# Two places of their own for the output tiles of the last stage, a four-place weight ring, and an earlier split of the last block's rows

## The chip, the cores and the metric

The kernel runs on one core of a Trainium2 chip. The metric is device time in microseconds (us). Before the change three timed runs gave 866.95, 863.05 and 864.15, median 864.15.

## The reference, cut to what matters

The program is one chain: attention (a coarse one and a local one, summed), a mixture of eight experts with one expert per token, and a two-layer feed-forward. Only the last link is touched:

```python
# x: 2304 tokens x 512; w_in: 512 x 2048; w_out: 2048 x 512
h = x @ w_in
g = np.maximum(h, 0.0) + alpha * np.minimum(h, 0.0)
out = g @ w_out                       # 2304 x 512, float32
```

## The kernel before, in words

**Precision.** Each float32 operand is split in a high and a low part (`split`: ScalarE casts the high part, VectorE or GpSimd subtracts it), and a product is three matmuls, high*high, high*low, low*high.

**Blocks.** The last stage (`moe2`) takes the tokens in blocks 0 to 3 of 512 and block 4 of 256. For each of 16 slices f of the hidden width it makes h (128 hidden columns x tokens) in a PSUM bank, applies the activation on VectorE (`act`: two instructions over the bank, into a tile m), splits the result into gh and gl, and later multiplies these by w_out into Y, four PSUM tiles of 128 tokens x 512 (`second`, 12 matmuls of 512 columns per slice, queued in `queue` and taken out by `run`). Blocks 0 and 1 are `plain`, block 4 is `end`.

**Blocks 2 and 3** (`sevens`) use seven half-size products instead of eight. Two slices make a pair; pairs q = 0 to 15 run through both blocks, p = q mod 8. A pair has seven products of six matmuls of 256 columns, into three banks: A ("11", then "S2", "S3", "22" added in turn, ScalarE copying the bank out after each), B ("12") and C ("S1", then "S4" added). Their parts meet in two tiles h0 and h1, which are activated and split like the others; q5 holds a copy of C.

**The weight ring.** S1 to S4 are sums of parts of w_in. During block 1, `Split7.make` computes them for p = 0 to 7 (tiles S1m and so on) and writes them to DRAM (`sd`); `Split7.fetch` loads them for each pair (S1r and so on, 256 KB each). Both draw their tiles from one ring of five places (`ring`): place i mod 5, in the order S1, S2, S4, S3. So a tile takes the place of the tile five before it: S2r of pair 0 that of S1m of p = 7. SyncE issues stores and fetches in one queue, in order, and a fetch waits there until its place is free.

**The output.** When the last slice of a token tile is added, `leave` copies Y from PSUM to a tile o (even tiles ScalarE, odd ones VectorE), and GpSimd issues an indirect DMA that writes the 128 rows to their tokens. The four DMAs of a block run one after the other, each issued when the one before has landed. The o tiles come from `mt`, the ring "m" with four places, which also holds every m, h0, h1, ma and mb: after a block's end these find their places taken by o tiles until the DMAs land.

**Other tiles.** `c64` gives a staging tile of 128 x 256 in turn from pool `ep`, tag "L", and pool `wst`; q5 comes from it. `plain_x` splits the token rows of block 4 into xf. In the source it stands after all pairs, ahead of the last pair's last product; its places in xf are free when the last pair has done "12".

**What sets the order.** The source is not the order of the instructions: a scheduler with its own forecast of times orders them per engine, and each engine then runs its list in order. Names with a number (h0, oy) lose it in the rows of the trace.

Of the kernel before, what the change touches and what calls it, by code (L numbers as in the profile page):

```python
# [5 lines left out]
F32=mybir.dt.float32; F32R=mybir.dt.float32r; BF16=mybir.dt.bfloat16; I32=mybir.dt.int32; U32=mybir.dt.uint32  # L6
# [538 lines left out]
def split(nc, hi, lo, x, lo_engine):  # L545

    nc.scalar.copy(hi,x)  # L547
    return lo_engine.tensor_tensor(out=lo,in0=x,in1=hi.bitcast(F32),op=ALU.subtract)  # L548
# [198 lines left out]
SKEW=48  # L747
BLOCKS=[(512*j,512) for j in range(4)]+[(2048,256)]
SEVEN=(2,3)
# [38 lines left out]
def moe2(tc, stack, wp, tp, xf, ep, win, wst, c64, W2out, W2in, al, ysT, ytok, sd, out, first):  # L788
    nc=tc.nc
    op=stack.enter_context(tc.tile_pool(name="o_const",bufs=1))  # L790
# [5 lines left out]
    wir,wil=win  # L796
    nring=itertools.count()
    def ring(name):
        i=next(nring)%5
        pool,tag,n=(wst,"raw64",3) if i<3 else (op,"s2",2)  # L800
        return pool.tile([128,2,2,128],F32R,tag=tag,name=name,bufs=n)
    seven=Split7(tc,ring,sd,win)
    def mt(name): return wk.tile([128,512],F32,tag="m",name=name,bufs=4)
    def bank(i,name): return hp.tile([128,512],F32,tag=f"h{i}",name=name)
    def gtiles(j,f):
        return wk.tile([128,512],F32R,tag="gh",name=f"gh{j}_{f}",bufs=LAG+1),wk.tile([128,512],F32R,tag="gl",name=f"gl{j}_{f}",bufs=LAG+1)
    G0=[gtiles(0,0)]; M0=[mt("m0_0")]
    xk=wk.tile([128,XW],F32R,name="xk",bufs=1)
    xin={}; Y={}; queue=[]; numbers={0:first[1]}
    def run(n):  # L810
        for _ in range(min(n,len(queue))): queue.pop(0)()
    def second(j,t,f,gh,gl,ts=None):
        ts=slice(128*t,128*t+128) if ts is None else ts
        for k,(a,b) in enumerate(((gh,woh),(gh,wol),(gl,woh))):
            nc.tensor.matmul(Y[j][t],lhsT=a[:,ts],rhs=b[:,f],start=f==0 and k==0,stop=f==15 and k==2)  # L815
        if f==15: leave(j,t)
    def leave(j,t):
        o=mt(f"o{j}{t}"); ti=numbers[j]
        if t%2: nc.vector.tensor_copy(o,Y[j][t])
        else: nc.scalar.copy(o,Y[j][t])  # L820
        nc.gpsimd.indirect_dma_start(out=out[:],out_offset=bass.IndirectOffsetOnAxis(ap=ti[:,t:t+1],axis=0),in_=o[:],in_offset=None,bounds_check=N-1,oob_is_err=False)  # L821
    def follow(j,f,gh,gl):
        for t in range(4): queue.append(lambda t=t: second(j,t,f,gh,gl))
    def accum(j): Y[j]=[yp.tile([128,DM],F32,tag="y",name=f"oy{j}{t}") for t in range(BLOCKS[j][1]//128)]
    def act(f,g,m,h,n=512):
        nc.vector.tensor_scalar(out=m[:,:n],in0=h[:,:n],scalar1=0.0,scalar2=al[:,f:f+1],op0=ALU.min,op1=ALU.mult)  # L826
        nc.vector.scalar_tensor_tensor(out=g[:,:n],in0=h[:,:n],scalar=0.0,in1=m[:,:n],op0=ALU.max,op1=ALU.add)  # L827

    raws={}
    def load_x(j):  # L830
        r0,n=BLOCKS[j]
        a=ep.tile([128,2,512],F32,tag="eh",name=f"oTa{j}",bufs=1); b=[ep.tile([128,512],F32,tag=t,name=f"oT{t}{j}",bufs=1) for t in ("T","eo")]
        raws[j]=[a[:,0],a[:,1],b[0],b[1]]
        for c in range(4): tc.keep_in_program_order(nc.sync.dma_start(raws[j][c][:,:n],ysT[128*c:128*c+128,r0:r0+n]))
        numbers[j]=ti=row_numbers(tc,tp,ytok,j)
        return a
    def plain_x(j,x,at):
        n=BLOCKS[j][1]
        hi=x[:,at:at+4*n].rearrange("p (c t) -> p c t",c=4); lo=x[:,at+4*n:at+8*n].rearrange("p (c t) -> p c t",c=4)
        for c in range(4): split(nc,hi[:,c],lo[:,c],raws[j][c][:,:n],nc.vector)  # L840
        xin[j]=(hi,lo)
    def place(x,i): return x[:,512*i+SKEW:512*i+SKEW+512].rearrange("p (c t) -> p c t",c=2)
    PLACES={"11":(0,0),"21":(0,2),"T1":(0,4),"T2":(0,6),"22":(1,0),"T3":(1,2),"T4":(1,4)}
    def seven_x(j,a,name):
        R=raws[j]; t1=slice(0,256); t2=slice(256,512); two=nc.gpsimd.tensor_tensor
        x,i=PLACES[name]
        if name=="11" and j>SEVEN[0]: x,i=1,6
        hi,lo=place((xf,xk)[x],i),place((xf,xk)[x],i+1)
        if name=="T1": two(out=a[:,:,t1],in0=a[:,:,t2],in1=a[:,:,t1],op=ALU.subtract)
        if name=="T3":  # L850
            for c in range(2): two(out=a[:,c,t2],in0=R[2+c][:,t2],in1=a[:,c,t2],op=ALU.subtract)
        if name=="T2":
            for c in range(2): two(out=a[:,c,t1],in0=R[2+c][:,t2],in1=a[:,c,t1],op=ALU.subtract)
        if name=="T4":
            for c in range(2): two(out=R[2+c][:,t1],in0=R[2+c][:,t1],in1=a[:,c,t1],op=ALU.subtract)
        if name in ("11","T1","T2"): split(nc,hi,lo,a[:,:,t1],nc.vector)
        elif name=="T3": split(nc,hi,lo,a[:,:,t2],nc.vector)
        else:
            for c in range(2): split(nc,hi[:,c],lo[:,c],R[2+c][:,t2 if name=="22" else t1],nc.vector)
        xin[j,name]=(hi,lo)  # L860
# [31 lines left out]
    def product(q,p,j,w,x,o,start,stop):  # L892
        W=seven.weight(q if w in seven.SUMS else p,w); xh,xl=xin[j,x]
        k=0
        for c in range(2):
            for a,b in ((0,xh),(0,xl),(1,xh)):
                nc.tensor.matmul(o[:,:256],lhsT=W(a,c),rhs=b[:,c],start=start and k==0,stop=stop and k==5,skip_group_check=True); k+=1  # L897
    def sevens():
        last=None
        for q in range(8*len(SEVEN)):  # L900
            j=SEVEN[0]+q//8; p=q%8; nxt=j+1 if p==7 else None
            if p==0: accum(j)
            if q+1<8*len(SEVEN): seven.fetch(q+1,(q+1)%8)
            if p==4: held.append(load_x(j+1))
            def x_for(name,nxt=nxt):
                if nxt in SEVEN: seven_x(nxt,held[-1],name)
            A=bank(q%2,f"pA{q}"); B=bank(2,f"pB{q}"); C=bank(3,f"pC{q}")
            if p==6 and j+1 in SEVEN: seven_x(j+1,held[-1],"11")
            product(q,p,j,"11","11",A,True,False)
            h0=mt(f"h0{q}"); h1=mt(f"h1{q}"); q5=c64(f"q5{q}",[128,256])  # L910
            nc.scalar.copy(h0[:,:256],A[:,:256])
            if last: last()
            run(4)
            product(q,p,j,"12","21",B,True,True)
            nc.vector.tensor_tensor(out=h0[:,:256],in0=B[:,:256],in1=h0[:,:256],op=ALU.add)
            x_for("21")
            product(q,p,j,"S1","T1",C,True,False)
            nc.scalar.copy(q5,C[:,:256])
            x_for("T1")
            product(q,p,j,"S2","T2",A,False,False)  # L920
            nc.scalar.copy(h0[:,256:],A[:,:256])
            x_for("T2")
            run(2)
            product(q,p,j,"S4","22",C,False,True)
            nc.vector.tensor_tensor(out=h0[:,256:],in0=C[:,:256],in1=h0[:,256:],op=ALU.add)
            gh,gl=gtiles(j,2*p)
            act(2*p,h0,mt(f"ma{q}"),h0); split(nc,gh,gl,h0,nc.vector); follow(j,2*p,gh,gl)
            x_for("22")
            product(q,p,j,"S3","T3",A,False,False)
            nc.scalar.copy(h1[:,256:],A[:,:256])  # L930
            nc.vector.tensor_tensor(out=h1[:,256:],in0=q5,in1=h1[:,256:],op=ALU.add)
            x_for("T3")
            run(2)
            def last(q=q,p=p,j=j,A=A,h1=h1,x_for=x_for):
                product(q,p,j,"22","T4",A,False,True)
                nc.scalar.copy(h1[:,:256],A[:,:256])
                gh,gl=gtiles(j,2*p+1)
                act(2*p+1,h1,mt(f"mb{q}"),h1); split(nc,gh,gl,h1,nc.vector); follow(j,2*p+1,gh,gl)
                x_for("T4")
        j=SEVEN[-1]+1  # L940
        plain_x(j,xf,SKEW)
        last(); run(4)
    def end(j):
        r0,n=BLOCKS[j]; xh,xl=xin.pop(j); accum(j); ts=slice(0,128); H=[]
# [14 lines left out]
        for f in range(16): second(j,1,f,zh[:,f],zl[:,f],ts)  # L959
    xin[0]=first[0]  # L960
    plain(0); plain(1); sevens(); end(4)

def row_numbers(tc, tp, ytok, j):
# [8 lines left out]
def body(tc,q,k,v,mod,wg,bias,w1,w2,w_in,w_out,alpha,out):  # L972
    nc=tc.nc
    with ExitStack() as ctx:
# [91 lines left out]
        with ExitStack() as s2:  # L1066
            moe2(tc,s2,wp,rp,xf,ep,(wir,wil),wst,c64,W2out,lambda f: W2in(24+f,1),al,ysT,ytok,sd,out,first)
# [26 lines left out]
```

## Time and profile before

| what | value |
|---|---|
| median of three runs | 864.15 us (863.05 to 866.95) |
| profiled execution | 859.76 us |
| its span, first to last instruction | 858.0 us |
| PE busy | 798.7 us (93%) |
| VectorE, ScalarE, GpSimd busy | 582.4, 402.7, 227.0 us (68%, 47%, 26%) |
| mean granted TensorE clock | 0.981 |

PE is TensorE's matmuls, DVE VectorE, ACT ScalarE, POOL GpSimd, SPq SyncE's queue of DMA issues. A busy PE is an engine that has a matmul in flight.

### The profile page before, as it was taken

What the parts mean: (1) busy time and instruction counts of PE and PEld (TensorE: products, weight loads), DVE (VectorE), ACT (ScalarE), POOL (GpSimd) and SP (SyncE); (2) the same over time, 40 slices, a digit from 0 to 9 for tenths busy, and PEclk for the clock granted to TensorE, in tenths of its full rate; (3) what the DMA queues carried; (4) which work ended last, traced back from release to release, by engine and by line L of the source; (5) the groups of instructions that cost most, each with busy time, mean ns of one, the idle gap of its engine ahead of it and who ended that gap; (6) DMA issues with size and microseconds to landing.
All of it is one profiled execution on the core that took longest, in us unless ns stands there. A gap on an engine that the chain in (4) does not pass through costs nothing.

```text
span 858.0 us, 18117 instructions
## 1 busy us (share of the span) xinstructions
PE 798.7 (93%) x6535; PEld 699.9 (82%) x6535; DVE 582.4 (68%) x1489; ACT 402.7 (47%) x987; POOL 227.0 (26%) x420
## 2 busy tenths in 40 slices
PE   4799899999998999989999999999999999899996
PEld 3477777778898999989998877788888988799895
DVE  6866856547525789988849999598845565445472
ACT  7697786885422665665532232233323233233220
POOL 9425556347431001101002224433410110100010
PEclk9989999989999999999999999999999999999999
DMA  7645675322313533469203343133262533342000
GB/s 193 170 109 159 190 217 148 90 53 56 80 52 87 88 100 84 94 124 285 83 26 118 116 159 112 74 144 126 99 228 92 160 109 113 103 119 87 13 38 25
DMA packets 110439, 96.99 MB, mean 113 GB/s; under 512 B 41992, under 2 KB 85512, under 8 KB 110344
## 3 DMA queue, kind: packets, MB, share of 16 engines
q1 hardware_dynamic: 107368, 86.19, 36.2%
q0 software_dynamic: 2976, 9.59, 3.2%
q8 instruction: 53, 0.87, 0.5%
q14 instruction: 42, 0.34, 0.2%
HBM read 93.21 MB, written 27.29 MB: 140 GB/s over the span
## 4 chain that ended last, share of the span: by engine, by line
PE 24%; DVE 14%; issue 14%; DMA 10%; ACT 2%; POOL 1%; SPq 1%; POOLq 0%; DVEq 0%; ACTq 0%
PE oy L815 7%; PE h L719 5%; PE y L739 5%; DMA out<-o,tt 5%; PE pA L897 3%; DMA wo<-in_moe_w_out 2%; PE oh L951 2%; DVE m L826 2%; DMA L<-xs 1%; DVE gl L548 1%; DVE m L827 1%; PE pC L897 1%; DVE sa L778 1%; DMA oTa<-ysT 1%; DVE w1l L548 1%
## 5 line engine op out<-in xcount | busy, mean ns | idle before, releaser
L815 PE MATMUL oy<-woh,gh 128*128 128x512 f32 x272 | 104.9, 394 | 6.5 <-ACT gh L547 3.3
L815 PE MATMUL oy<-wol,gh 128*128 128x512 f32 x272 | 106.4, 391 | 0.8 <-POOL wol L548 0.8
L815 PE MATMUL oy<-woh,gl 128*128 128x512 f32 x272 | 96.6, 390 | 0.0
L719 PE MATMUL h<-xh,w1h 128*128 128x256 f32 x224 | 63.5, 284 | 6.8 <-DVE hl L722 6.8
L815 PEld LDWEIGHTS oy<-woh,gh 128*128 128x128 f32 x272 | 50.9, 188 | 18.0 <-ACT woh L547 4.9
L719 PE MATMUL h<-xh,w1l 128*128 128x256 f32 x224 | 63.1, 282 | 0.0
L719 PE MATMUL h<-xl,w1h 128*128 128x256 f32 x224 | 63.1, 282 | 0.0
L547 ACT CAST gh<-m 128x512 fp32r<-128x512 f32 (+1 forms) x48 | 24.7, 514 | 80.3 <-DVE m L827 78.1
L739 PE MATMUL y<-hh,w2h 128*128 128x256 f32 x224 | 61.0, 280 | 0.0
L739 PE MATMUL y<-hh,w2l 128*128 128x256 f32 x224 | 60.5, 280 | 0.0
L815 PEld LDWEIGHTS oy<-wol,gh 128*128 128x128 f32 x272 | 51.1, 188 | 10.4 <-POOL wol L548 1.7
L739 PE MATMUL y<-hl,w2h 128*128 128x256 f32 x224 | 58.8, 281 | 0.7 <-DVE hl L722 0.7
L815 PEld LDWEIGHTS oy<-woh,gl 128*128 128x128 f32 x272 | 50.4, 188 | 10.1 <-DVE gl L548 0.4
L548 POOL TENSOR_TENSOR wol<-xwo,woh 128x256 fp32r<-128x256 f32 x32 | 25.1, 789 | 109.0 <-ACT woh L547 64.4
L821 POOL DMA_INDIRECT out<-o,tt x18 | 18.5, 1025 | 131.6 <-ACT o L820 96.2
L719 PEld LDWEIGHTS h<-xh,w1h 128*128 128x128 f32 x224 | 42.7, 191 | 8.0 <-DVE hl L722 8.0
L547 ACT CAST w1h<-wraw 128x512 fp32r<-128x512 f32 x56 | 34.0, 620 | 30.3 <-PE h L719 22.7
L602 PE MATMUL py<-eh,wraw 128*128 128x128 f32 x320 | 43.7, 288 | 4.1 <-SPq L1059 3.4
L579 POOL TENSOR_TENSOR L<-L 128x1024 f32<-128x1024 f32 x7 | 14.4, 2061 | 120.3 <-DMA L<-xs 99.0
L602 PE MATMUL ph<-Te,wraw 128*128 128x128 f32 x320 | 44.9, 292 | 0.0
L602 PEld LDWEIGHTS py<-eh,wraw 128*128 128x128 f32 x320 | 39.5, 199 | 5.9 <-SPq L1059 3.6
L719 PEld LDWEIGHTS h<-xl,w1h 128*128 128x128 f32 x224 | 42.8, 191 | 0.0
(373 smaller groups left out, 2289.9 us busy)
## 6 DMA issues: line engine op xcount, KB each, us to landing
wraw<-in_moe_w SPq DMA_DIRECT2D x56, 512.0 KB
wi<-in_moe_w_in SPq DMA_DIRECT2D x32, 256.0 KB
wo<-in_moe_w_out SPq DMA_DIRECT2D x32, 256.0 KB
vw<-in_v SPq DMA_DIRECT2D x88, 64.0 KB
xs<-z SPq DMA_DIRECT2D x8, 528.0 KB
ldq<-in_q SPq DMA_DIRECT2D x16, 256.0 KB
ldk<-in_k SPq DMA_DIRECT2D x16, 256.0 KB
ldv<-in_v SPq DMA_DIRECT2D x8, 512.0 KB
```

The source lines that it names most:

```text
L547: nc.scalar.copy(hi,x)
L548: return lo_engine.tensor_tensor(out=lo,in0=x,in1=hi.bitcast(F32),op=ALU.subtract)
L579: nc.gpsimd.tensor_tensor(out=L[:,:,:128],in0=L[:,:,:128],in1=L[:,:,128:129].to_broadcast([128,g,128]),op=ALU.mult)
L602: nc.tensor.matmul(get(key),lhsT=lhsT,rhs=rhs,start=first,stop=last)
L719: nc.tensor.matmul(h,lhsT=a[:,c],rhs=b[:,c],start=n==0,stop=n==11); n+=1
L739: nc.tensor.matmul(y,lhsT=a[:,f],rhs=b,start=n==0,stop=n==23); n+=1
L778: nc.vector.tensor_tensor(out=o,in0=x,in1=y,op=op)
L815: nc.tensor.matmul(Y[j][t],lhsT=a[:,ts],rhs=b[:,f],start=f==0 and k==0,stop=f==15 and k==2)
L821: nc.gpsimd.indirect_dma_start(out=out[:],out_offset=bass.IndirectOffsetOnAxis(ap=ti[:,t:t+1],axis=0),in_=o[:],in_offset=None,bounds_check ...
L826: nc.vector.tensor_scalar(out=m[:,:n],in0=h[:,:n],scalar1=0.0,scalar2=al[:,f:f+1],op0=ALU.min,op1=ALU.mult)
L897: nc.tensor.matmul(o[:,:256],lhsT=W(a,c),rhs=b[:,c],start=start and k==0,stop=stop and k==5,skip_group_check=True); k+=1
L951: nc.tensor.matmul(h[:,:n],lhsT=a[:,c,fs],rhs=b[:,c],start=k==0,stop=k==11); k+=1
```

## The change

The o tiles leave the ring "m" and take in turn two places of their own: one new, in pool `op`, tag "L", and one in pool `ep`, tag "L". The weight ring has four places instead of five (i mod 4: S1, S2 and S4 rotate in pool `wst`, S3 has its own in `op`); a tile now takes the place of the tile of the same name one pair before. q5 has one place, in `wst`. The split of block 4's rows is called inside the last pair, after "12", ahead of the products S1, S2, S4 and S3, behind which it stood before.

```diff
     def ring(name):
-        i=next(nring)%5
-        pool,tag,n=(wst,"raw64",3) if i<3 else (op,"s2",2)
+        i=next(nring)%4
+        pool,tag,n=(wst,"raw64",3) if i<3 else (op,"s3",1)
         return pool.tile([128,2,2,128],F32R,tag=tag,name=name,bufs=n)
     seven=Split7(tc,ring,sd,win)
+    nout=itertools.count()
+    def ot(name): return (op,ep)[next(nout)%2].tile([128,512],F32,tag="L",name=name,bufs=1)
...
     def leave(j,t):
-        o=mt(f"o{j}{t}"); ti=numbers[j]
+        o=ot(f"o{j}{t}"); ti=numbers[j]
...
-            h0=mt(f"h0{q}"); h1=mt(f"h1{q}"); q5=c64(f"q5{q}",[128,256])
+            h0=mt(f"h0{q}"); h1=mt(f"h1{q}"); q5=wst.tile([128,256],F32,tag="c64",name=f"q5{q}",bufs=1)
...
             x_for("21")
+            if nxt and nxt not in SEVEN: plain_x(nxt,xf,SKEW)
...
-        j=SEVEN[-1]+1
-        plain_x(j,xf,SKEW)
         last(); run(4)
```

Three places of the engines' lists follow, where a number behind a name is its pair or slice (S2m7: S2 for p = 7; S2r0: its fetch for pair 0; o12: block 1, token tile 2; h10: h1 of pair 0).

**Place A, the end of block 1.** VectorE, before:

```order
L548 TENSOR_TENSOR S1m7_14202<-sa71_14196,S1m7_14202 128x256
L548 TENSOR_TENSOR xk_12703<-oTeo2_13933,xk_12703 128x256
L778 TENSOR_TENSOR sa70_14194<-sa70_14194 128x256
L548 TENSOR_TENSOR xk_12703<-oTeo2_13933,xk_12703 128x256
L548 TENSOR_TENSOR S2m7_14203<-sa70_14194,S2m7_14203 128x256
L826 TENSOR_SCALAR m1_15_14251<-oh1_15_14238,al_64 128x512
```

VectorE, now:

```order
L548 TENSOR_TENSOR S1m7_14202<-sa71_14196,S1m7_14202 128x256
L548 TENSOR_TENSOR xk_12703<-oTeo2_13933,xk_12703 128x256
L778 TENSOR_TENSOR sa70_14194<-sa70_14194 128x256
L548 TENSOR_TENSOR S3m7_14205<-sa71_14196,S3m7_14205 128x256
L548 TENSOR_TENSOR xk_12703<-oTeo2_13933,xk_12703 128x256
L828 TENSOR_SCALAR m1_15_14251<-oh1_15_14238,al_64 128x512
L548 TENSOR_TENSOR S2m7_14203<-sa70_14194,S2m7_14203 128x256
```

S3m7 has moved ahead and S2m7 behind the activation of block 1's last slice. SyncE's queue at the same place, before:

```order
L782 DMA sd_60<-S1m7_14202 128x512
L786 DMA S1r0_14218<-sd_60 128x512
L782 DMA sd_60<-S2m7_14203 128x512
L786 DMA S2r0_14220<-sd_60 128x512
L782 DMA sd_60<-S4m7_14204 128x512
L782 DMA sd_60<-S3m7_14205 128x512
L786 DMA S4r0_14222<-sd_60 128x512
L786 DMA S3r0_14224<-sd_60 128x512
```

SyncE, now:

```order
L782 DMA sd_60<-S1m7_14202 128x512
L782 DMA sd_60<-S3m7_14205 128x512
L786 DMA S1r0_14218<-sd_60 128x512
L782 DMA sd_60<-S2m7_14203 128x512
L786 DMA S3r0_14224<-sd_60 128x512
L782 DMA sd_60<-S4m7_14204 128x512
L786 DMA S2r0_14220<-sd_60 128x512
L786 DMA S4r0_14222<-sd_60 128x512
```

The fetch S2r0 stood two rows behind the store whose place it took (S1m7); it now takes the place of S2m7, whose store is later.

**Place B, the copies of block 1's output.** ScalarE, before:

```order
L820 COPY o10_14357<-oy10_13567 128x512
L930 COPY h10_14318<-pA0_14308 128x256
L547 CAST gh2_0_14377<-h00_14317 128x512
L820 COPY o12_14395<-oy12_13569 128x512
L918 COPY xq51_14427<-pC1_14418 128x256
```

ScalarE, now:

```order
L822 COPY o10_14357<-oy10_13567 128x512
L822 COPY o12_14395<-oy12_13569 128x512
L933 COPY h10_14318<-pA0_14308 128x256
L913 COPY h01_14425<-pA1_14416 128x256
L547 CAST gh2_0_14377<-h00_14317 128x512
L921 COPY q51_14427<-pC1_14418 128x256
```

The copy o12, which takes the place that o10 leaves, stands right behind it, ahead of h10 and the cast gh2_0.

**Place C, the first slices of block 4.** VectorE, before:

```order
L819 COPY o31_16070<-oy31_15154 128x512
L819 COPY o33_16086<-oy33_15156 128x512
L826 TENSOR_SCALAR m4_1_16104<-oh4_1_16091,al_64 128x256
L827 SCALAR_TENSOR_TENSOR m4_1_16104<-oh4_1_16091,m4_1_16104 128x256
L548 TENSOR_TENSOR gl4_1_16108<-m4_1_16104,gh4_1_16107 128x128
```

VectorE, now:

```order
L821 COPY o31_16070<-oy31_15154 128x512
L828 TENSOR_SCALAR m4_1_16104<-oh4_1_16091,al_64 128x256
L828 TENSOR_SCALAR m4_2_16129<-oh4_2_16116,al_64 128x256
L828 TENSOR_SCALAR m4_3_16154<-oh4_3_16141,al_64 128x256
L829 SCALAR_TENSOR_TENSOR m4_1_16104<-oh4_1_16091,m4_1_16104 128x256
L829 SCALAR_TENSOR_TENSOR m4_2_16129<-oh4_2_16116,m4_2_16129 128x256
L829 SCALAR_TENSOR_TENSOR m4_3_16154<-oh4_3_16141,m4_3_16154 128x256
...
L821 COPY o33_16086<-oy33_15156 128x512
```

The copy o33 has gone from the second row to behind the activations of slices 1 to 4 (eleven rows are left out).

## Rows read from the trace of the kernel before

**Rows 1.** Busy time by stretch: columns as in its first line.

```profile
core 0: us, PE busy (x) PEld busy (x) DVE busy (x) ACT busy (x) POOL busy (x), PEclk, DMA share, GB/s
...
640.00:650.00 10.00, 6.99 (x40) 5.98 (x40) 5.47 (x11) 2.48 (x6) 2.28 (x2) 1.00 0.39 127
650.00:720.00 70.00, 70.00 (x443) 63.14 (x442) 37.94 (x68) 22.78 (x56) 7.09 (x8) 1.00 0.40 118
720.00:740.00 20.00, 15.69 (x99) 13.52 (x98) 9.03 (x17) 5.86 (x14) 4.33 (x4) 1.00 0.48 145
740.00:810.00 70.00, 70.00 (x444) 63.48 (x443) 32.52 (x64) 19.46 (x47) 0.18 (x1) 1.00 0.25 72
810.00:820.00 10.00, 8.63 (x55) 7.50 (x54) 6.12 (x16) 2.57 (x8) 2.92 (x3) 1.00 0.16 68
```

**Rows 2.** Waits of PE, 540 to 850: us in total, times, longest.

```profile
PE oy L815 <- ACT gh L547: 3.3, 2, 2.7
PE oh L951 <- DVE m L827: 1.4, 1, 1.4
PE pA L897 <- ACT h L930: 1.2, 1, 1.2
PE pA L897 <- ACT h L911: 1.2, 1, 1.2
PE pC L897 <- DMA S4r<-sd: 1.2, 1, 1.2
PE oy L815 <- DVE o L819: 0.4, 1, 0.4
```

**Rows 3.** Timeline, block 1's end: start, us, engine, [idle before <-releaser].

```profile
630.93 1.01 POOL L821 DMA_INDIRECT out<-o,tt  x1 [14.11 <-ACT o L820]
...
634.77 0.37 ACT L930 COPY h<-pA 128x256 f32<-128x256 f32 x1 [4.12 <-DMA out<-o,tt]
...
639.70 0.69 DVE L819 COPY o<-oy 128x512 f32<-128x512 f32 x1 [3.10 <-DMA out<-o,tt]
...
643.15 0.48 DVE L826 TENSOR_SCALAR mb<-h,al 128x512 f32<-128x512 f32 x1 [2.43 <-DMA out<-o,tt]
```

**Rows 4.** Timeline, block 2's end.

```profile
720.70 1.01 POOL L821 DMA_INDIRECT out<-o,tt  x1 [12.97 <-ACT o L820]
...
725.37 0.97 POOL L821 DMA_INDIRECT out<-o,tt  x1 [3.67 <-DMA out<-o,tt]
...
728.52 0.37 ACT L911 COPY h<-pA 128x256 f32<-128x256 f32 x1 [3.62 <-DMA out<-o,tt]
...
729.94 0.32 SPq L786 DMA_DIRECT2D S4r<-sd  x1
...
733.24 0.94 PE L897 MATMUL pC<-xk,S4r 128*128 128x256 f32 x6 [1.19 <-DMA S4r<-sd]
```

**Rows 5.** Timeline, block 3's end.

```profile
814.01 0.48 DVE L826 TENSOR_SCALAR m<-oh,al 128x256 f32<-128x256 f32 x1 [2.06 <-DMA out<-o,tt]
```

**Rows 6.** Timeline, the last sums stored and pair 0's fetched.

```profile
622.37 0.32 SPq L782 DMA_DIRECT2D sd<-S1m  x1
...
623.26 0.41 DVE L548 TENSOR_TENSOR S2m<-sa,S2m 128x256 fp32r<-128x256 f32 x1
...
623.60 0.74 DVE L826 TENSOR_SCALAR m<-oh,al 128x512 f32<-128x512 f32 x1
...
623.71 0.32 SPq L782 DMA_DIRECT2D sd<-S2m  x1
...
624.35 0.32 SPq L786 DMA_DIRECT2D S2r<-sd  x1
...
625.30 0.32 SPq L782 DMA_DIRECT2D sd<-S4m  x1
...
628.44 0.87 PE L897 MATMUL pA<-xf,S2r 128*128 128x256 f32 x6
...
628.72 0.32 SPq L786 DMA_DIRECT2D S3r<-sd  x1
...
632.57 0.87 PE L897 MATMUL pC<-xk,S4r 128*128 128x256 f32 x6
```

## The prediction, made before the changed kernel ran

> **What bounds the kernel now.** I read the share of busy time first: TensorE is busy 93% of the span at a mean clock of 0.981, VectorE 68%, so a change in the last stage can only win the time in which PE stands there. Next comes the table by stretches [rows 1]. The reader is to look at the PE column against the width: between the blocks' ends PE is busy 70.00 of 70.00 us; around them it is idle 10.00 - 6.99 = 3.01 us, 20.00 - 15.69 = 4.31 and 10.00 - 8.63 = 1.37, in all 8.69. The clock stands at 1.00 in every one of these stretches, so nothing is to be had from it. The list of PE's waits from 540 to 850 us [rows 2] gives the same by name: 3.3 + 1.4 + 1.2 + 1.2 + 1.2 + 0.4 = 8.7. So all of PE's idle time there is accounted for, and it lies behind three block ends.
>
> Those waits name ScalarE and VectorE, which are far from full, so the third view is the timeline there, for what held them. At block 1's end ScalarE's copy h idles 4.12 us, VectorE's copy o 3.10 and its activation mb 2.43, and each is released by an output DMA [rows 3]. At block 2's end it is GpSimd 3.67 and ScalarE 3.62 [rows 4], at block 3's VectorE 2.06 [rows 5]. The code says why: o, m, ma, mb, h0 and h1 share a ring of four, the output DMAs run one behind the other, and h or m must wait until an o tile is written out. A DMA takes 634.77 - 630.93 = 3.8 us from issue to the release [rows 3], or 725.37 - 720.70 = 4.7 and 728.52 - 725.37 = 3.2 [rows 4]. The sixth wait is another kind: a fetch S4r issued at 729.94 and used at 733.24, 3.3 us later, with PE waiting 1.19 for it [rows 4]. It was issued late because its place in the ring of five was that of the S2r of the pair before.
>
> **What the change removes.** With o tiles in places of their own no m or h tile waits for an output DMA. That covers 8.7 - 1.2 = 7.5 us. The S4r wait (1.2) should go as well: with four places a fetch takes the place of its own name one pair earlier. In the changed order the shortest way from a product to the same product of the next pair is 42 matmuls, and a matmul takes on average 70.00/443 = 0.158 us [rows 1], so 42 of them, most of 256 columns, take at most 6.6 and, as shorter ones, perhaps 5.5 us (an estimate); the fetch needs 3.3. If both go entirely, 8.7 us are won.
>
> **Added, first: pair 0's fetch.** Place A shows it. S2r0 waited before for the store of S1m, issued at 622.37, and was issued itself at 624.35; PE used it at 628.44 [rows 6] without a wait in [rows 2]. Now it waits for the store of S2m, and S2m stands behind the activation on VectorE. Step by step: S2m began at 623.26 and its store was issued 0.45 later, at 623.71; behind an activation, 0.74 us by its row, some of it overlapped, S2m begins near 624.26 and the store is issued near 624.71. How long until a store releases a place: 624.35 - 622.37 = 2.0 in one case, 628.72 - 625.30 = 3.4 in the other [rows 6]; I take 2.7. How long a fetch takes: 3.3 [rows 4]. So S2r0 is in at 624.71 + 2.7 + 3.3 = 630.7, and PE, due at 628.44, waits 2.3 us. Bounds: with 2.0 for both it is 628.7, a wait of 0.3; with 3.4 and the longest DMA above, 4.7, it is 632.8, a wait of 4.4. The other fetches of pair 0 are not late: S3r0 moves ahead, and S4r0, behind a store issued near 625.3 that needs 3.4 and then 3.3, is in at 632.0, ahead of its use at 632.57 [rows 6], which the wait before it moves back to 634.9.
>
> The rows show 2.0 to 3.4 us for a store and 3.3 for a fetch of 256 KB [rows 4, 6]. The Trainium skill ("DMA: Bandwidth & Descriptors", section "Anatomy of one DMA — SWDGE (gpsimd) path") gives about 2.0 us plus the bytes over 436 GB/s, fitted on GpSimd's DMAs, which these are not; as an estimate from that page each of the two would take 2.6 us, S2r0 would be in at 629.9 and PE would wait 1.5, 0.8 us less than my sum has. The fetch in this kernel measures longer, so the measurement decides.
>
> **Added, second: copies that wait for a place.** With two places, o2 waits for the first DMA of its block and o3 for the second, and they wait at the head of ScalarE's and VectorE's lists. At block 1's end o12 stands ahead of h10 (Place B). The first DMA lands at 634.77 [rows 3], just when h10's copy ran before; now o12's copy comes first, at 0.69 us by VectorE's row for the same copy [rows 3], and h10 is late by that. The cost for PE lies between 0 and 0.69; I take 0.35. The copy o13 needs the second DMA, some 3.8 us later, 638.6; before, it came at 639.70, so the 0.4 of [rows 2] is not exceeded, and I let it go. At block 2's end the same two landings, 725.37 and 728.52 [rows 4], hold o22 and o23. The cost lies between 0 and 2.4, the two ScalarE waits of 1.2 that stand there today [rows 2]; only one copy's time is left by the same reasoning as at block 1, so 0.55. At block 3's end o33 is behind the activations of four slices (Place C), and only a later copy is late: 0, at most the 1.4 that PE waits for VectorE's m now [rows 2]. Together 0.9, with bounds 0 and 0.69 + 2.4 + 1.4 = 4.5.
>
> **Added, third.** q5 in one place and the earlier call of the split: taken at 0. The scheduler had the instructions of the split between the same pairs' work already, PE waits for neither q5 nor xf in [rows 2], and VectorE is busy 32.52 of 70.00 us in block 3 [rows 1], which covers them. If the cover failed, the nearest rows are the 1.2 of a late ScalarE copy [rows 2] for the one and four subtractions of half a tile, 4 x 0.41 = 1.6 by S2m's row [rows 6], for the other. A gain of as much isn't to be had, since nothing waits there. The work of block 4 after 840 us is unchanged: 0.
>
> **The sum.** 8.7 - 2.3 - 0.9 = 5.5 us less. Against the profiled execution, 859.76, that is 854.3. The median of the three timed runs is 4.4 above that execution; I take the whole offset over: 864.15 - 5.5 = 858.6, or 0.64% less. With the bounds, 8.7 - 0.3 - 0 = 8.4 at best and 8.7 - 4.4 - 4.5 - 2.8 = -2.8 at worst, if all bad ends met.
>
> **Rivals.**
>
> *A full gain.* The store and the fetch of S2r0 are as quick as the quicker rows, and the copies hide. For it: the 2.0 us between 622.37 and 624.35; against it: the fetch measured at 3.3. Time: 864.15 - 8.4 = 855.8.
>
> *The waits come back under new names.* The output DMAs still run one after the other, so the copies o2 and o3 come when they did, and what stands behind them on ScalarE and VectorE is late as before: half of the 7.5 comes back. For it: ScalarE's list at Place B has o12 ahead of h10, and the landings set the times in [rows 3, 4]. Against: the longest waits, those behind mb and m [rows 3, 5], were for the third and fourth place, which no instruction but a copy needs now. Time: 864.15 - (8.7 - 3.75 - 2.3) = 861.5.
>
> *The ring of four becomes the bound: slower.* Each fetch can be issued only when the same product of the pair before is done, 5.5 to 6.6 us ahead of its use. It decides from the point where a fetch takes longer than that. There are 16 pairs; at some 15 places in them the way is that short. If the fetches take 7.5 us, each of these costs 1 to 2 us, some 20 in all, and the time is 864.15 - 5.5 + 20 = 878; below 10 us in all it doesn't come out slower. Against it: 3.3 us is the fetch that PE was seen waiting for, the longest DMA in these rows is 4.7, and the DMA share is 0.25 to 0.48 [rows 1].
>
> *It does not do what it says.* The places are free, but PE's idle time at the block ends has another cause, such as the activation's own way from the product to gh. Against it: the releasers in [rows 3 to 5] are DMAs, not engines. Time: about 864, or 866 with the wait for S2r0.
>
> **How the numbers follow.** The forecast, 858.6, has a chance of 0.5, and its own range is 857 to 861. A full gain has 0.13, the waits under new names 0.22, the ring as a bound 0.06, no effect 0.09. A difference of 0.5%, 4.3 us, is about what a measurement of this kernel can tell from no change, so faster is below 859.8 and slower above 868.5. Faster holds the full gain and most of the forecast (0.13 + 0.45), and little of the rest: 0.58. Slower is the ring's case and a small part of the last: 0.08. The same is what remains, 0.34. The range runs from 855.0 to 864.5: it takes in the full gain, the waits under new names and half of no effect.
>
> **What would show it.** In the changed kernel's table by stretches PE should stand near 10 of 10 us behind each block's end. No h, m or mb should be released by an output DMA; the copies o2 and o3 should be, with idle times of 3 to 4 us. The first PE wait should be for S2r near 628 to 631, 2.3 us long, released by its DMA, and no later S1r to S4r should hold PE. The forecast is wrong if PE still waits more than 2 us in sum for ScalarE's or VectorE's rows at the block ends, if it waits for fetches in many pairs, or if the stretches between the ends (70.00 of 70.00 today) have idle time.

## The result and the profile after

The changed kernel took 851.56 us (median, 849.10 to 854.04) against 864.13 for the one before: ratio 0.9857, interval 0.9821 to 0.9893, 12.6 us less. The forecast was 858.6 and its range began at 855.0, so the sign was right and the size less than half of what came. A second comparison with more runs gave 850.22 against 862.87, ratio 0.9851 (0.9813 to 0.9889).

First the table by stretches of the changed kernel, to be held against [rows 1]; the block ends come 1.1, 3.4 and 10.0 us earlier, so that of block 3 now begins in the stretch 740 to 810.

```profile
core 0: us, PE busy (x) PEld busy (x) DVE busy (x) ACT busy (x) POOL busy (x), PEclk, DMA share, GB/s
...
640.00:650.00 10.00, 10.00 (x64) 9.01 (x63) 5.77 (x12) 3.62 (x8) 1.32 (x2) 1.00 0.40 130
650.00:720.00 70.00, 69.13 (x437) 62.47 (x437) 40.12 (x72) 24.08 (x57) 8.10 (x9) 1.00 0.40 121
720.00:740.00 20.00, 20.00 (x128) 18.09 (x128) 10.12 (x19) 5.95 (x14) 3.08 (x3) 1.00 0.47 145
740.00:810.00 70.00, 70.00 (x446) 63.50 (x444) 35.33 (x77) 20.55 (x54) 3.14 (x4) 1.00 0.25 78
810.00:820.00 10.00, 10.00 (x76) 9.49 (x75) 6.79 (x20) 2.50 (x10) 1.09 (x1) 1.00 0.12 43
```

PE is busy through all three block ends. The only idle time left, 70.00 - 69.13 = 0.87 us, is a new wait, in the middle of block 2 (the cast xk waits for the load of block 3's rows, and gh is a cast that stands behind it):

```profile
679.85 0.62 ACT L547 CAST xk<-oTa 128x512 fp32r<-128x512 f32 x1 [4.61 <-DMA oTa<-ysT]
...
683.38 0.62 ACT L547 CAST gh<-h 128x512 fp32r<-128x512 f32 x1 [2.09 <-DVE h L829]
...
684.05 0.50 PE L817 MATMUL oy<-woh,gh 128*128 128x512 f32 x1 [0.87 <-ACT gh L547]
```

ScalarE stood 4.61 us for the load of block 3's rows, and PE waited 0.87 us for the cast gh; the run with the rows loaded a pair earlier, below, shows that the first brought the second.

The timeline around block 1's end in the changed kernel answers to [rows 3] and [rows 6].

```profile
620.37 0.42 DVE L548 TENSOR_TENSOR S2m<-sa,S2m 128x256 fp32r<-128x256 f32 x1
...
620.92 0.38 SPq L782 DMA_DIRECT2D sd<-S2m  x1
...
623.91 0.32 SPq L786 DMA_DIRECT2D S2r<-sd  x1
...
627.29 0.93 PE L899 MATMUL pA<-xf,S2r 128*128 128x256 f32 x6
...
629.82 1.01 POOL L823 DMA_INDIRECT out<-o,tt  x1 [16.99 <-ACT o L822]
...
632.65 0.59 ACT L822 COPY o<-oy 128x512 f32<-128x512 f32 x1 [3.10 <-DMA out<-o,tt]
```

The fetch S2r waits for S2m's store, as forecast, but PE does not wait for the fetch. The copy o12 waits for the first output DMA, as forecast, and no one waits for the copy.

Since the two profiled executions also differ by 1.2 us ahead of the first output DMA, where the code is the same, I measure the last stage from the issue of that DMA to the end of the span. These are its rows, of the kernel before and then of the changed kernel:

```profile
541.05 1.04 POOL L821 DMA_INDIRECT out<-o,tt  x1 [1.74 <-ACT o L820]
```

```profile
539.86 1.04 POOL L823 DMA_INDIRECT out<-o,tt  x1 [1.69 <-ACT o L822]
```

So the stage took 858.0 - 541.05 = 316.95 us and takes 847.4 - 539.86 = 307.5: 9.4 us less. The experiments below use this length, which comes out within 0.2 us in two executions of the changed kernel. Each length is that of one profiled execution. All of them, with PE's waits from the first output DMA on:

| kernel | first output DMA | span | length | PE waits of the stage |
|---|---|---|---|---|
| before | 541.05 | 858.0 | 316.95 | block ends, S4r 1.2 |
| before, 2nd to 4th execution | 540.97, 535.62, 544.55 | 859.6, 857.3, 862.7 | 318.6, 321.7, 318.2 | block ends, S4r 0.9 to 1.4 |
| changed | 539.86 | 847.4 | 307.5 | gh 0.9 |
| changed, 2nd execution | 534.63 | 842.3 | 307.7 | gh 0.9 |
| ring of four alone | 536.99 | 856.2 | 319.2 | block ends, gh 0.9, S2r 0.9, S4r 1.4 |
| block 0's o in ring m | 536.81 | 845.0 | 308.2 | S2r 1.3 |
| split of block 4 late | 537.72 | 845.6 | 307.9 | gh 0.9 |
| rows loaded a pair earlier | 540.50 | 847.5 | 307.0 | DVE h 0.3 |
| one o place, ring of four | 541.56 | 852.9 | 311.3 | S2r 2.9, S4r 0.3 |
| one o place, ring of five | 545.73 | 853.7 | 308.0 | DVE h 1.7 |

### The profile page after: what moved, and what is told of

Read it like the earlier page. It is cut to its first block, busy times and chain, and to the rows that moved or that the text cites. A ratio compares the mean times of both kernels' runs of the same rounds, so it can differ in the third digit from the quotient of the medians.

```text
span 847.4 us, 18115 instructions
## 1 busy us (share of the span) xinstructions
PE 795.5 (94%) x6535; PEld 699.2 (83%) x6535; DVE 579.1 (68%) x1489; ACT 404.2 (48%) x987; POOL 226.5 (27%) x420
## 4 chain that ended last, share of the span: by engine, by line
PE 47%; DVE 8%; DMA 5%; issue 3%; ACT 2%; POOL 1%; SPq 1%; POOLq 0%; DVEq 0%; ACTq 0%
PE oy L817 18%; PE h L719 6%; PE y L739 6%; PE oh L874 5%; PE pA L899 5%; PE oh L952 3%; PE pC L899 2%; DMA wo<-in_moe_w_out 2%; DMA L<-xs 1%; PE pB L899 1%; DMA oTa<-ysT 1%; DVE xwo L557 1%; DVE xwo L556 1%; DVE xwo L555 1%; DVE w1l L548 1%
## 5 line engine op out<-in xcount | busy, mean ns | idle before, releaser
L548 DVE TENSOR_TENSOR w1l<-wraw,w1h 128x512 fp32r<-128x512 f32 x56 | 38.3, 691 | 7.9 <-ACT w1h L547 7.7
L719 PEld LDWEIGHTS h<-xh,w1l 128*128 128x128 f32 x224 | 43.3, 193 | 0.0
```

The costliest lines, as they stand in the source:

```text
L719: nc.tensor.matmul(h,lhsT=a[:,c],rhs=b[:,c],start=n==0,stop=n==11); n+=1
```

## The experiments

**The changed kernel again.** No edit.

> The changed kernel again, more rounds. Its matmuls stand 9.35 us less than before's between 540 and 850 us (10.50 against 1.15 by the starts of the matmuls in the two traces); the other 1.15 us by which the two profiled executions differ arose ahead of 540 us, where the code is the same. If only that counts, the ratio comes out at 0.989 (9.4 us less). Rival: the 12.6 us between the first medians are real and something outside the last stage got quicker too: ratio 0.9855.

Measured: 0.9851 (0.9813 to 0.9889), the length 307.7 us. So the timed gain of 12.6 came a second time. The 9.4 of the two first traces, 0.989 as a ratio, is inside the first interval and just outside the second. What is missing is looked for in the kernel before, below.

**The ring of four alone.**

```diff
-        i=next(nring)%5
-        pool,tag,n=(wst,"raw64",3) if i<3 else (op,"s2",2)
+        i=next(nring)%4
+        pool,tag,n=(wst,"raw64",3) if i<3 else (op,"s3",1)
```

> The kernel before with the ring of four places alone; o tiles stay in the ring of m. Theory (the gain is the o tiles'): the block-end waits of PE stay at 7 to 8 us in the list, the wait for S4r (1.2) goes, and since VectorE is still held at the end of block 0 by the first output DMA, S2m of p = 7 is as late as the prediction had it: a wait of PE for S2r of pair 0 of 1.5 to 2.3 us appears. Time within 1.5 us of before. Rival (the ring of four brings a good part of the gain, by earlier fetches): 3 us or more faster, with block-end waits shorter.

Measured: ratio 1.0002 (0.9972 to 1.0032), length 319.2. The block-end waits are still there, 6.0 us of them (I expected 7 to 8), S2r's has appeared (0.94, where I expected 1.5 to 2.3), and the wait for S4r has not gone. So the ring of four alone brings none of the gain, and the expectation for S4r failed. This is the list of PE's waits in that kernel:

```profile
PE oy L815 <- ACT gh L547: 4.0, 3, 2.5
PE pC L897 <- DMA S4r<-sd: 1.4, 1, 1.4
PE oh L951 <- DVE m L827: 1.4, 1, 1.4
PE pA L897 <- ACT h L911: 1.2, 1, 1.2
PE pA L897 <- DMA S2r<-sd: 0.9, 1, 0.9
PE pA L897 <- ACT h L930: 0.2, 1, 0.2
```

The three waits for gh hold two at the block ends and one of 0.85 at 684.27, the new wait of the changed kernel, which is thus there without the change of the o tiles. Counted from the first output DMA, S2m starts at 81.3 us, behind a stop of VectorE of 3.02 us at block 0's end; in the kernel before it starts at 82.2, behind a stop of 3.03 (row below, in the account of the prediction):

```profile
618.30 0.42 DVE L548 TENSOR_TENSOR S2m<-sa,S2m 128x256 fp32r<-128x256 f32 x1
```

**Block 0's o tiles back in the ring m**, on top of the changed kernel.

```diff
-        o=ot(f"o{j}{t}"); ti=numbers[j]
+        o=(ot if j else mt)(f"o{j}{t}"); ti=numbers[j]
```

> The changed kernel, but block 0's four o tiles stay in the ring of m. Theory (pair 0's fetch came in time only because VectorE no longer stood 3.0 us at the end of block 0): VectorE waits about 3 us for an output DMA again near 550, runs some 2.7 us later through block 1, S2m of p = 7 starts near 623, and PE waits for S2r of pair 0 by 1.0 to 2.3 us (626.5 + 2.7 against 627.3 when it is due); 1 to 2.3 us slower than the changed kernel. Rival (S2r0 would have been in time anyway, as stores and fetches are quicker than the prediction had them): no such wait, same time as the changed kernel.

Measured: length 308.2, 0.7 more than the changed kernel; the timing can't tell that (0.9848, 0.9805 to 0.9890). The rows show VectorE held again, S2m's start, its store, the fetch, and PE's wait:

```profile
546.62 0.75 DVE L828 TENSOR_SCALAR m<-oh,al 128x512 f32<-128x512 f32 x1 [3.03 <-DMA out<-o,tt]
...
618.08 0.42 DVE L548 TENSOR_TENSOR S2m<-sa,S2m 128x256 fp32r<-128x256 f32 x1
...
618.64 0.38 SPq L782 DMA_DIRECT2D sd<-S2m  x1
...
622.01 0.32 SPq L786 DMA_DIRECT2D S2r<-sd  x1
...
625.61 0.94 PE L899 MATMUL pA<-xf,S2r 128*128 128x256 f32 x6 [1.25 <-DMA S2r<-sd]
```

The wait of 1.25 is in the range expected, but not for the whole reason given. Counted from the first output DMA, S2m starts at 81.3 us here and at 80.5 in the changed kernel: 0.8 us of VectorE's stop of 3.0 reached S2m, not 2.7. In the changed kernel VectorE stands too at that place, 3.3 us for PE's oh, so part of the stop takes the place of another. The other part is a chain that was longer, 625.61 - 618.08 = 7.5 us from S2m's start to PE's use. The gh wait is gone in this kernel, so the net, 0.7, is smaller than the wait.

**The split of block 4's rows at its old place.** `plain_x` is called after all pairs again.

> The changed kernel with the split of block 4's rows called where it was before, after all pairs. Theory (the move costs and brings nothing, as the prediction had it): within 1 us of the changed kernel. Rival (between the first output DMAs of blocks 2 and 3 the changed kernel gained 6.6 us, of which the waits there explain 5.2: the rest is the move): 1.4 us slower or more, with PE idle near 800 to 815.

Measured: length 307.9 and ratio 0.9841 (0.9803 to 0.9878). The move costs and brings nothing that shows. From the first output DMA of block 2 to that of block 3 it is 83.90 us in both kernels, so the part of the 6.6 us that the waits don't explain had another cause: o30's copy now stands a little earlier in the order (43 of block 4's matmuls oh begin ahead of it, 51 in the kernel before).

**Block 3's rows loaded a pair earlier.** `if p==4: held.append(load_x(j+1))` becomes `if p==3: ...`.

> The changed kernel with the load of the next block's token rows called at pair 3 of a block and not at pair 4. Theory (the one wait that is left, 0.9 us of PE for a cast gh near 683, comes from ScalarE standing 4.6 us for the load of block 3's rows, issued at 674.95 behind a fetch that waits for its place): the load goes out some 10 us earlier, the wait goes, 1.0 us less than the changed kernel from the first output DMA to the end (307.5 to 306.5). Rival: the load holds back the fetches of pair 5 or collides with others, a wait for S1r to S4r takes its place, no gain.

Measured: the load goes out at 663.42 and not at 674.95, the gh wait is gone, the length is 307.0, 0.5 to 0.7 less. A wait of 0.3 for VectorE's h remains. It is the shortest stage of all, but the timing (0.985, 0.9807 to 0.9894) does not tell it from the changed kernel.

**One place for all o tiles**, with the ring of four, and then with the ring of five.

```diff
-    def ot(name): return (op,ep)[next(nout)%2].tile([128,512],F32,tag="L",name=name,bufs=1)
+    def ot(name): return ep.tile([128,512],F32,tag="L",name=name,bufs=1)
```

> The changed kernel with one place for all o tiles (early pool alone). Copies then wait for each DMA of the block in turn, 3.5 to 4.7 us apart, at the head of ScalarE's and VectorE's lists. Theory (two places are enough to hide the copies, one is not): PE waits at the three block ends for the copies o2 or o3 or for what stands behind them, 3 to 8 us in sum; from the first output DMA to the end 310 to 316 us against 307.5. Rival (the scheduler puts the copies where they cost nothing, the number of places doesn't matter): within 1 us of 307.5.

Measured: length 311.3, and no PE wait for a copy or for what stands right behind one. PE's waits from 535 us on, of which those for woh and wol lie ahead of the first output DMA:

```profile
PE pA L899 <- DMA S2r<-sd: 2.9, 1, 2.9
PE oy L817 <- ACT woh L547: 1.1, 2, 0.7
PE oy L817 <- POOL wol L548: 0.8, 2, 0.5
PE pC L899 <- DMA S4r<-sd: 0.3, 1, 0.3
```

The length is in the expected range, but not for the reason given: no block end costs PE anything at a copy. What costs is that VectorE stands at block 0's end for a copy o, 5.23 us, so that S2m starts at 624.85 - 541.56 = 83.3 us behind the first output DMA, and its fetch is 2.9 us late. So a waiting copy does cost, but nearly 90 us later and by another tile. The clock adds to the length: right behind that wait it was 0.50 (last row). The rows:

```profile
544.47 0.69 DVE L821 COPY o<-oy 128x512 f32<-128x512 f32 x1 [5.23 <-DMA out<-o,tt]
...
624.85 0.42 DVE L548 TENSOR_TENSOR S2m<-sa,S2m 128x256 fp32r<-128x256 f32 x1
...
632.01 1.61 PE L899 MATMUL pA<-xf,S2r 128*128 128x256 f32 x6 [2.93 <-DMA S2r<-sd]
```

```profile
632.00:635.40 3.40, 3.39 (x11) 3.02 (x12) 0.00 (x0) 0.84 (x2) 0.00 (x0) 0.50 0.53 178
```

> As the one with a single place for o tiles, but with the ring of five for the weights as before. It tells whether the S4r wait of the kernel before was the ring's or followed from the o tiles: the kernel with the ring of four alone still had a wait of 1.4 for S4r. Theory (it followed from PE's stops at the block end): no wait for S1r to S4r here either, and the same waits for copies as with the ring of four. Rival (the ring of five has its own late fetch): a wait for S4r of about 1 us at the start of block 3.

Measured: length 308.0, no wait for any of S1r to S4r. So the S4r wait of [rows 4] was not the ring's: at the start of block 3 it was there with five places and with four while o tiles lay in the ring m, and with neither once they did not (the 0.3 in the list above stands elsewhere, at 642.41). With the ring of five the late S2m is harmless too, since S2r0 takes another place. The half of the expectation on copies came true here, in one place: VectorE stands 7.01 us for a place for o at block 1's end, and PE waits 1.66 us for the tile h right behind that copy:

```profile
640.13 0.69 DVE L821 COPY o<-oy 128x512 f32<-128x512 f32 x1 [7.01 <-DMA out<-o,tt]
640.74 0.41 DVE L928 TENSOR_TENSOR h<-pC,h 128x256 f32<-128x256 f32 x1
...
641.21 0.97 PE L899 MATMUL pC<-xf,S1r 128*128 128x256 f32 x6 [1.66 <-DVE h L928]
```

So one extra place for o, with the weight ring as it was, did nearly all of the work in this one execution; the changed kernel, with two places, has no wait behind a copy.

**The kernel before, three more executions.** No edit.

> The kernel before against itself. It shows what the timing can tell: ratio 1.000, with the interval's half width. It also reads the time ahead of the last stage a second time: the profile before had the first output DMA at 541.05 us, the other runs of the same code up to there have it at 534.6 to 539.9. If that was chance, it lands in this range now and the last stage's length, from this DMA to the end, is 317 us as before (316.95); if the kernel before is slower ahead of the stage for a reason, it is at 541 again.

Measured: ratio 0.9999 (0.9971 to 1.0026), so 0.3% is what the timing tells. The first output DMA is at 540.97, the rival's sign, but at 535.62 and 544.55 in the next two: its place varies. But the length is 318.6, not 317. The table by stretches of this execution shows why, right behind the stops at the ends of blocks 1 and 2:

```profile
641.00:644.70 3.70, 1.10 (x10) 0.90 (x8) 1.18 (x2) 0.58 (x2) 1.22 (x2) 0.97 0.44 148
644.70:648.00 3.30, 3.21 (x8) 2.56 (x9) 2.48 (x5) 0.93 (x3) 0.17 (x1) 0.52 0.19 79
732.00:736.00 4.00, 2.10 (x17) 1.73 (x16) 1.87 (x4) 0.99 (x2) 1.30 (x1) 1.00 0.77 244
736.00:740.00 4.00, 3.57 (x9) 2.37 (x10) 1.42 (x3) 0.74 (x2) 0.09 (x1) 0.58 0.40 139
```

PE is busy in the second and fourth row, but at a granted clock of 0.52 and 0.58: most of it at the lower level, 1.2 GHz. In its timeline the matmuls of 512 columns follow each other 0.43 us apart:

```profile
644.78 0.79 PE L815 MATMUL oy<-woh,gh 128*128 128x512 f32 x1 [2.69 <-ACT gh L547]
645.38 0.63 PE L815 MATMUL oy<-wol,gh 128*128 128x512 f32 x1
645.80 0.63 PE L815 MATMUL oy<-woh,gh 128*128 128x512 f32 x1
646.23 0.63 PE L815 MATMUL oy<-wol,gh 128*128 128x512 f32 x1
```

The execution that the prediction rests on had the same stop, and went on at full clock, 0.23 us apart:

```profile
642.19 0.28 PE L897 MATMUL pB<-xf,wil 128*128 128x256 f32 x1
645.12 0.50 PE L815 MATMUL oy<-woh,gh 128*128 128x512 f32 x1 [2.66 <-ACT gh L547]
645.46 0.39 PE L815 MATMUL oy<-wol,gh 128*128 128x512 f32 x1
645.69 0.39 PE L815 MATMUL oy<-woh,gh 128*128 128x512 f32 x1
```

> A third look at the kernel before, for one question: in the second look TensorE's granted clock fell to 0.52 and 0.58 in two stretches of 3 to 4 us right behind the stops at the ends of blocks 1 and 2, in the first it stayed at 1.00. If the clock falls behind such stops by chance, this look has it or not, and the last stage (first output DMA to the end) is 316.5 to 319.5 us accordingly, against 307.5 for the changed kernel; that would put the change's worth between 9.4 and 12 us. Rival (the second look was a rare exception): clock 1.00 here, 317.0 us.

> A fourth look at the kernel before, for the same question: clock level behind the stops at the block ends, and the last stage's length, 316.5 to 319.5 us if the clock falls by chance, 317.0 if it stays at 1.00.

Measured: 321.7 and 318.2. In the first of them the clock fell behind block 1's stop, as its table by stretches shows:

```profile
639.00:643.00 4.00, 1.34 (x8) 0.96 (x7) 2.23 (x5) 0.89 (x2) 1.31 (x1) 1.00 0.44 153
643.00:646.50 3.50, 3.50 (x13) 3.07 (x12) 1.97 (x4) 1.14 (x3) 0.00 (x0) 0.53 0.06 23
```

And one output DMA came late. Issued at 631.31, it let go of VectorE's copy o at 636.51, 5.2 us later, and PE waited 1.39 for that copy:

```profile
631.31 1.00 POOL L821 DMA_INDIRECT out<-o,tt  x1 [4.33 <-DMA out<-o,tt]
...
636.51 0.69 DVE L819 COPY o<-oy 128x512 f32<-128x512 f32 x1 [4.26 <-DMA out<-o,tt]
...
637.26 0.50 PE L815 MATMUL oy<-woh,gh 128*128 128x512 f32 x1 [1.39 <-DVE o L819]
```

In the second the clock stayed up, as this row behind block 1's stop (2.65 us) shows, and the waits were longer by 1.1 in sum:

```profile
649.00:652.00 3.00, 2.82 (x15) 2.48 (x16) 2.20 (x4) 0.93 (x3) 0.27 (x1) 1.00 0.21 87
```

So the range given (316.5 to 319.5) was too narrow, and the clock doesn't decide the length alone, as I expected: the waits vary too. The mean length of the four executions is 318.85; the changed kernel's is 307.6. The difference, 11.2 us, lies within the interval of the second timed comparison, 9.6 to 16.1 us; it rests on four executions against two, not all on one chip.

## Why the prediction was right or wrong

**What bounds the kernel, and what the change removes: right in kind, too small in size.** No h, m or mb waits for an output DMA in the changed kernel, and the S4r wait is gone. But 8.7 us was the sum of the idle times that the rows list, and a stop costs more than its row says. At 642.19 PE's last matmul ahead of a stop begins; matmuls of 256 columns begin 0.12 us apart, so the next was due at 642.31 and began at 645.12, a loss of 2.81 where the row has 2.66, and the matmul behind it began 0.34 later and not 0.23. Adding up in this way all starts of matmuls from 541 to 850 us gives about 10.5 us for the kernel before, and about 1.15 for the changed one (its gh wait of 0.87). The difference, about 9.35, accounts for the 9.4 by which the stage is shorter. The Trainium skill says of TensorE ("Perfetto Trace Analysis", section "Tensor Engine Instruction (MATMUL, LD_WEIGHTS)") that the profiler estimates where a matmul ends. The rows can't show that; they show that a listed end lies 0.16 us behind the next one's start, so that listed idle time begins 0.16 us later than PE could have begun a matmul.

**Why S4r's wait went: wrong reason.** It was put down to the ring of five. The runs show that it went with the o tiles: with them in the ring m it stayed in a ring of four, without them it was absent in a ring of five. That PE's own stops are the link between the two was not tried by itself.

**Added, first (2.3 us for pair 0's fetch): the step that failed.** What was measured is 0. The mechanism is real (0.9, 1.3 and 2.9 us in three experiments), and the mistake is in the second number of the chain: "S2m begins near 624.26", which is 83.2 us behind the first output DMA. It began at 80.5. I took the time of S2m before and added one activation, as if VectorE's work ahead of it stayed where it was. Two things moved that work. One is VectorE's stop of 3.0 us for an m tile at block 0's end, which the prediction leaves out, as PE did not wait there. This is its row in the kernel before:

```profile
550.86 0.75 DVE L826 TENSOR_SCALAR m<-oh,al 128x512 f32<-128x512 f32 x1 [3.03 <-DMA out<-o,tt]
```

0.8 us of it reached S2m, by the run with block 0's o tiles in the ring m. The other is the new order of VectorE's list, the remaining 1.9: the kernel with the ring of four alone has the stop and S2m at 81.3 all the same, so this part comes with the ring. What in that order does it was not tried. The three kernels that waited show how near it was: S2m at 81.3, 81.3 and 83.3 us behind the first DMA gave waits of 0.9, 1.3 and 2.9; at 80.4 to 80.5, in three kernels, PE waits 0 to 0.2. With my 83.2 the wait would have been near the 2.9 of the last of these, more than my 2.3: from S2m's start to PE's use they took 7.2 to 7.5 us, where my chain had 0.45 + 2.7 + 3.3 = 6.45.

**Added, second (0.9 us for the copies): failed as well, 0 measured.** The copies wait as predicted (o12 3.10 us) and with two places nobody waits behind them, so the rival on waits under new names falls. Its mechanism exists: with a single place PE waited 1.66 us behind a copy at one block end. No fetch holds PE in the changed kernel, so the rival of the ring as a bound falls too.

**Added, third (0): right** for the split, by the run with it at its old place. The single place of q5 was not tried by itself; PE nowhere waits for it. The load of the next block's rows, which the prediction didn't consider, gave a new wait of 0.9, and the load one pair earlier removed it.

**The sum, and one execution.** 8.7 - 3.2 = 5.5 was forecast. The terms as measured are 10.5 - 1.15 = 9.35: 3.2 more, as two terms came out at 0, and some 0.7 more from the stops' true price less the new wait. Part of the rest, 11.2 - 9.4 = 1.8 us of 3.2, lies in the kernel before: the execution that the sum was made against was, by chance, the shortest of four in this stage (316.95 against 318.2, 318.6 and 321.7). Carrying its offset to the median over unchanged assumed that what makes an execution slower than the profiled one is untouched by the change. It wasn't, in these executions: part of it happened at the stops that the change removed. So did the sentence that nothing was to be had from the clock fail: it read 1.00 in that one execution, and 0.52 to 0.58 behind the same stops in two others. The rivals' prices had the same flaw; the full gain, 855.8, was the nearest and still 4 us too long. (Two slips in the prediction's sums decide nothing: its worst end is -3.0 and not -2.8, and the ring's case is 879 and not 878.)

**What is still open.** Timed 12.6 against 11.2 in the lengths is inside the interval and isn't explained further. How often the clock falls behind a stop isn't known from four executions.

## What to carry to other kernels

A wait that PE doesn't feel can still hold an engine whose backlog sets a much later deadline; before a moved instruction is given its old time plus what it was moved behind, the engine's waits ahead of it have to be taken off. A stop's price is read from the starts of the matmuls on both sides, not from the listed idle time. And where executions differ, a second and third profile of the kernel before says whether the part that varies is the part that is about to be removed.

## What the runs showed of the hardware

Behind stops of PE of 2.5 to 2.9 us TensorE's granted clock fell in some executions and not in others: 0.52 behind 2.69 us idle, 0.53 behind 2.65, and 1.00 behind 2.66 and behind another 2.65, in the same kernel at the same place; where it fell it was back to 1.00 some 3 us later. The kernel with one o place and the ring of four shows it too: behind its wait of 2.93 us for S2r the clock was 0.50, and matmuls of 512 columns come 0.42 us apart. It also fell behind three shorter stops in a row, of 0.7 to 1.5 us, at block 2's end: to 0.58 in the second execution of the kernel before, and to 0.50 from 732.5 to 735.5 us in the kernel with the ring of four alone; the first execution had three such stops there too, of 0.7 to 1.2 us, and kept 1.00. Where it fell behind a single stop, the stop cost about half as much again: in the second execution the six matmuls from 645.38 to 647.92 took 2.54 us in place of 1.36. In the two executions of the changed kernel PE never stood longer than 0.9 us in this stage, and no matmul there began late but behind that wait. The Trainium skill says ("TensorE: Matmul & The Clock Gate", section "HAM oscillation — how this bites in real kernels") that idle gaps beyond a certain length bring the clock down and that the work behind them pays for it. The second execution agrees (0.52); the first shows that a stop of the same length need not do it (1.00).

The time from an output DMA's issue to the release of its place varied from 2.8 us (811.22 to 814.01, [rows 5] for the second) to 5.2 in the kernel before; the same DMA, the second of block 1, took 4.0 to 5.2 in its four executions.
